# VectorE adds up 28 of wq's 32 slices, wq comes in two halves, and TensorE's code is steered by a branch and a hint

## The chip, the cores and the metric

The kernel runs on one NeuronCore of one Trainium2 chip. The metric is the device time of one execution in microseconds. Engines are named as in the profile: PE is TensorE, DVE is VectorE, ACT is ScalarE, POOL is GpSimd, SP is SyncE; a q behind the name (SPq) is its instruction queue. All data are 32-bit floats.

## The reference

One decode step: a layer norm of one token, attention over a cache of 65,536 keys, and a two-layer network with relu beside it, all added to the input.

```python
B, Sq, D = 1, 1, 512
Hq, Hkv, Sk, Dh = 32, 8, 65536, 128          # four query heads share a key head
x  = A_x
xn = layernorm(x)
q  = (xn @ wq)                               # wq: [512, 4096], 8.4 MB
scores = q . k_cache * Dh**-0.5              # k_cache: [8, 65536, 128], 268 MB
o  = softmax(scores) . v_cache               # v_cache: the same size
attention = o @ wo                           # wo: [4096, 512], 8.4 MB
mlp = relu(xn @ w1) @ w2                     # 512 x 1792 and 1792 x 512, 3.7 MB each
return x + attention + mlp
```

## The kernel before

**Storage.** Two large buffers hold what comes from memory: `ks` for K tiles and `vs` for V tiles, 64 KB in each of 128 partitions, 8.4 MB each. They are used again for the weights: wq and later wo lie in `vs`, w1 and w2 in `ks`.

**The loads.** All large transfers are issued by SP on one queue, in this order: wq in two pieces (`WQ = [4, 28]`, slices of 512 columns; the helper is `load_slices`, L157), the first K tile (L175), the first V tile (L310), then K and V tiles in turn (L305, L310), four of each for every one of the 8 key heads, 32 of each in all; at the end w1 and w2 into `ks`, and wo into `vs` in seven pieces (`WO`). A V tile is issued when its semaphore `v_free` is raised. The first V tile overwrites wq, so SP waits (L319) for `wq_read`, the mark of the last matmul that reads wq.

**The head.** After the first loads are issued, the program of the helper context ends with a barrier of the engines (L179). Then VectorE, TensorE and ScalarE compute the layer norm (L210 to L230), some constant matrices (L234 to L249), and a spread form of xn: `pz`, a small matmul (L262), has the 128 x 32 numbers that belong to the 32 slices of wq. L264 multiplies them out to `xs`, 128 x 32 x 8, in which each slice's column stands at the place of its key head. wq is laid out with (head, 16 row groups) on the partitions and, for each of the 32 slices, 512 columns in the free dimension, so that

```python
pr[32 * c : 32 * c + HKV, :] += xs[:, i, :]^T @ vs[:, i * 512 : (i + 1) * 512]     # i = 0..31, c = i % 4
```

gives all query heads: 32 matmuls of 128x512 in 32-bit floats (L288), in four row groups c of one PSUM bank. `pr` is copied to `rows` (L295), turned by four transposes (L279) and summed over c into `qall` (L297). GpSimd hands each head its four queries in `qcur` (L336).

**The loop.** TensorE runs one loop of 32 passes (`STEPS`); a pass is one K tile (32 matmuls, L352), the maximum handling (L357 to L359), and one V tile (32 matmuls, L368). VectorE has a loop of 8 heads with four tiles written out in it (L384 to L423), ScalarE one of 8 heads with the exponentials (L430). VectorE raises `k_free` when the scores of a tile are read and `v_free` when a V tile's product is done. VectorE's loop is placed with `head_slot`, which fixes the slot of a code block at which its first instruction is loaded.

**The end.** TensorE multiplies by w1, w2 and wo (L451, L513, L548), VectorE transposes the result (L560), SP stores it. VectorE's last transpose stands in a loop that runs once (`last_turn`); its closing branch carries a hint that is placed ahead of VectorE's main loop (`end_hint`). Such a hint is an instruction that names a later branch.

**Order.** Each engine runs its program in the order written. `Flow.op` gives an instruction a wait for the marks it is handed and raises the engine's own semaphore; `DV.mark` is VectorE's latest mark.

Of the kernel before, what the change touches and what calls it, by code (L numbers as in the profile page):

```python
# [10 lines left out]
ALU = mybir.AluOpType  # L11
AX = mybir.AxisListType
PSUM = bass.MemoryType.PSUM
ENG = mybir.EngineType

P = 128
D = 512
HQ, HKV, DH = 32, 8, 128
# [3 lines left out]
CT = 4  # L22
# [11 lines left out]
FB = DFF // P  # L34
R = HKV
SLICES = R * G
WQ = [4, 28]
WO = [8, 8, 8, 4, 2, 1, 1]
PAIRED = 16
DIRECT = 28  # L40
# [29 lines left out]
def attention_and_mlp_kernel(  # L70
# [28 lines left out]
    nc = tc.nc  # L99
    scale = float(DH) ** -0.5  # L100
    te, ve, se, ge, sy = nc.tensor, nc.vector, nc.scalar, nc.gpsimd, nc.sync

    def place(name, *shape, rows=P):
        return nc.alloc_sbuf_tensor(name, [rows, *shape], F32).ap()
# [5 lines left out]
    vs = place("vs", NT * KEYS)  # L110
# [5 lines left out]
    mine = place("mine", HKV)  # L116
# [1 line left out]
    eighth = place("eighth", R)  # L118

    flat_tr = tr.rearrange("p b i -> p (b i)")  # L120
    xs = flat_tr[:, : SLICES * HKV].rearrange("p (i h) -> p i h", h=HKV)
    xm = flat_tr[:, SLICES * HKV : SLICES * (HKV + 1)]
    om, spread = flat_tr[:, : R * HQ], flat_tr[:, R * HQ : 2 * R * HQ].rearrange("p (r h g) -> p r h g", r=R, h=HKV)
    heads = flat_tr[:, 2 * R * HQ : 2 * R * HQ + 2 * DH]
    st = place("st", 8)
# [25 lines left out]
    PE, DV, AC, GP = (Flow(nc, e, n) for e, n in ((te, "pe"), (ve, "dve"), (se, "act"), (ge, "pool")))  # L151
# [3 lines left out]
    def load(engine, name, dst, src, n=16):  # L155
        sem = nc.alloc_semaphore(name)
        i = engine.dma_start(dst, src)  # L157
        i.then_inc(sem, n)
        if claim:
            claim(i)  # L160
        return sem, n


    def load_slices(name, src, counts):
        marks = []
        for n in counts:
            cut = slice(len(marks) * D, (len(marks) + n) * D)
            marks += [load(sy, f"{name}{len(marks)}", vs[:, cut], src[:, cut])] * n
        return marks


    if True:
        x_in = load(se, "x_in", xT, x.rearrange("(p a) -> p a", p=P))
        wq_in = load_slices("wq", wq.rearrange("h (i r) a f -> (h i) (r a f)", r=R), WQ)
        i = sy.dma_start(ks, k[0, 0, :, : NT * KEYS])  # L175
# [3 lines left out]
    tc.compile()  # L179
    claim = None  # L180


    make_identity_marks = []

# [7 lines left out]
    for t in (acc_o, acc_z, pm):  # L192
# [34 lines left out]
    DV.op(lambda e: e.tensor_mul(st[:, 6:7], st[:, 6:7], st[:, 3:4]), DV.mark)  # L227
    DV.op(lambda e: e.tensor_scalar(st[:, 6:7], st[:, 6:7], -0.5, 1.5, op0=ALU.mult, op1=ALU.add), DV.mark)
    DV.op(lambda e: e.tensor_mul(st[:, 7:8], st[:, 5:6], st[:, 6:7]), DV.mark)
    xn_in = DV.op(lambda e: e.tensor_scalar_mul(xn, xc, st[:, 7:8]), DV.mark)  # L230


# [27 lines left out]
    )  # L260
    pz = pb[:, 1, :]
    PE.op(lambda e: e.matmul(pz[:, :SLICES], octet, xm, start=True, stop=True), DV.mark)  # L262
    xs_in = DV.op(
        lambda e: e.tensor_mul(  # L264
            xs, pz[:, :SLICES].unsqueeze(2).to_broadcast([P, SLICES, HKV]),
            mine.unsqueeze(1).to_broadcast([P, SLICES, HKV]),
        ),
        PE.mark,
    )
    DV.op(lambda e: e.memset(idg, 1.0))  # L270
    DV.op(lambda e: e.tensor_copy(idg[:, :G], ident[:G, :G]), DV.mark)
# [1 line left out]
    pr, pt = pa[:, 0, :], pb[:, 0, :]  # L273
# [8 lines left out]
        return pt.rearrange("p (j c l) -> p j c l", j=4, c=CT)  # L282

    cleared = DV.op(lambda e: e.memset(pr, 0.0))
    for i in range(SLICES):
        c = i % CT
        PE.op(
            lambda e: e.matmul(  # L288
                pr[32 * c : 32 * c + HKV, :], xs[:, i, :], vs[:, i * 512 : (i + 1) * 512],
                start=(i < CT), stop=(i >= SLICES - CT),  # L290
            ),
            cleared, xs_in, wq_in[i],
        )
    wq_read = PE.mark
    DV.op(lambda e: e.tensor_copy(rows, pr), PE.mark)  # L295
    q = turn()[:, :, :, :HKV].rearrange("p j c h -> p h j c")
# [45 lines left out]
    GP.op(lambda e: e.tensor_copy(fins[:, HKV - 1, :], fin))  # L342


    with nc.Fori(0, STEPS, engines=[ENG.PE]):
        te.wait_ge(k_in, 16).then_inc(k_in, -16)
        te.wait_ge(q_in, 1).then_inc(q_in, -1)  # L347
        for s in range(NT):
            tile_of = (pa, pb)[s // 2 % 2][:, s % 2, :]
            for c in range(CT):  # L350
                at = (s * CT + c) * TW
                i = te.matmul(tile_of[32 * c : 32 * c + 32, :], qcur, ks[:, at : at + TW], start=True, stop=True)  # L352
                if c == 0 and s in (4, 6):
                    i._wait_ge(s_dve, s // 2 - 1)
            if s % 2:
                i.then_inc(s_tiles, 1)
        te.transpose(pm[:G, :P], m, ident)._wait_ge(s_dve, 3).then_inc(s_max, 1)  # L357
        te.matmul(pm[:, P : P + G], ones[:G, :], dg[:, :G], start=True, stop=True)._wait_ge(s_dve, 4)  # L358
        te.matmul(  # L359
            pm[:, P + G : P + G + 1], rowg, dg[:, G : G + 1], start=True, stop=True  # L360
        ).then_inc(s_max, 1)
        te.sem_inc(s_dve, -4)
        te.wait_ge(v_in, 16).then_inc(v_in, -16)
        te.wait_ge(s_w, 1).then_inc(s_w, -1)  # L364
        n = NT * SUB // WIDE
        for i in range(n):
            c = i % CT
            mm = te.matmul(  # L368
                acc_o[32 * c : 32 * c + WIDE * G, :],
                wt[:, i * WIDE : (i + 1) * WIDE, :].rearrange("p b g -> p (b g)"),  # L370
                vs[:, i * 512 : (i + 1) * 512],
                start=(i < CT), stop=(i >= n - CT),
            )
        mm.then_inc(s_o, 1)


    end_hint = ve.mark_branch_hint_location()
    with nc.Fori(0, HKV, engines=[ENG.DVE], head_slot={ENG.DVE: 110}):
        for n in range(NP):
            for s in range(0, NT, 2):  # L380
                if s == NT - 2:

                    ve.wait_ge(s_tiles, NT // 2).then_inc(k_free, 1)
                i = ve.transpose(  # L384
                    tr[:, s * SUB : (s + 2) * SUB, :].rearrange("p b i -> p (b i)"),
                    (pa, pb)[s // 2 % 2].rearrange("p i k -> p (i k)"),
                )._wait_ge(s_tiles, s // 2 + 1)
                if s < 4:
                    i.then_inc(s_dve, 1)
            ve.sem_inc(s_tiles, -4)  # L390
            ve.drain()
            top = m if n == 0 else mc
            i = ve.reduce_max(top, tr[:, :, :G].rearrange("p b g -> p g b"), axis=AX.X)  # L393
            if n:
                ve.drain()
                i = ve.tensor_max(m, m, mc)  # L396
            i.then_inc(s_dve, 1)
            ve.reduce_max(mg, pm[:G, :P], axis=AX.X)._wait_ge(s_max, 1)  # L398
            ve.drain()
            ve.tensor_scalar(dg, idg, mg, -scale, op0=ALU.mult, op1=ALU.mult).then_inc(s_dve, 1)  # L400
            ve.tensor_copy(bias[:, n, :], pm[:, P : P + G + 1])._wait_ge(s_max, 2).then_inc(s_bias, 1)  # L401
            ve.sem_inc(s_max, -2)
            flat = acc.rearrange("p b d -> p (b d)")
            if n:
                ve.wait_ge(s_alpha, 1).then_inc(s_alpha, -1)
            ve.wait_ge(s_o, 1).then_inc(v_free, 1)  # L406
            if n == 0:
                ve.tensor_copy(flat, acc_o)  # L408
            else:
                ve.scalar_tensor_tensor(  # L410
                    flat, flat, alpha[:, n : n + 1], acc_o, op0=ALU.mult, op1=ALU.add
                )
            ve.sem_inc(s_o, -1)
        ve.drain()
        last = bias[:, NP - 1, :G].unsqueeze(1).to_broadcast([P, NP - 1, G])
        ve.tensor_sub(diff, last, bias[:, : NP - 1, :G]).then_inc(s_diff, 1)
        ve.tensor_mul(masked, acc, selb.unsqueeze(2).to_broadcast([P, WIDE, DH]))
        ve.wait_ge(s_alpha, 1).then_inc(s_alpha, -1)
        ve.tensor_mul(part[:, : NP - 1, :], part[:, : NP - 1, :], fac)
        ve.wait_ge(f_free, 1).then_inc(f_free, -1)  # L420
        ve.drain()
        ve.reduce_sum(fin[:, DH:], part.rearrange("p n g -> p g n"), axis=AX.X)
        ve.reduce_sum(fin[:, :DH], masked.rearrange("p b d -> p d b"), axis=AX.X).then_inc(f_out, 1)  # L423


    with nc.Fori(0, HKV, engines=[ENG.Activation]):
        for n in range(NP):
            se.wait_ge(s_bias, 1).then_inc(s_bias, -1)  # L428
            for g in range(G):
                i = se.activation(  # L430
                    wt[:, :, g], tr[:, :, g], AF.Exp, bias=bias[:, n, g : g + 1],
                    scale=scale, accum_out=part[:, n, g : g + 1],
                )
# [13 lines left out]
    for a in range(A):  # L447
        for c in range(CT):
# [4 lines left out]
                    start=(a == 0), stop=(a == A - 1),  # L453
# [74 lines left out]
    for j in range(SLICES):  # L528
        if j == SLICES - 2:

            for c in range(CT):
# [3 lines left out]
                        start=False, stop=False,  # L535
# [9 lines left out]
        else:  # L545
            for c in range(CT):
# [3 lines left out]
                        start=False, stop=(j == SLICES - 1),  # L550
                    ),
                    sw_in, wo_in[j],
                )

    turns = nc.alloc_registers("turns", engines=[ENG.DVE])
    nc.regs_mov(turns, 0)
    nc.br("last_turn", engines=[ENG.DVE])
# [43 lines left out]
```

## Time and profile before

| | before |
|---|---|
| median of 3 runs | 1303.62 us (1303.43 to 1303.95) |
| the profiled execution | 1303.08 us |
| its span, first to last instruction | 1301.8 us |
| busy: PE, DVE, ACT, POOL | 657.1, 268.5, 76.0, 4.1 us |
| moved | 561.06 MB, mean 431 GB/s |
| wq, 7168 KB piece, issue to landing | 21.4 us |
| the 32 K loads and 32 V loads, issue to landing (median) | 29.1 us |

The profile is of one execution. Its span leaves out 1.28 us of the execution's time. Rows of a timeline read: start in us, duration in us, engine, line, operation, output<-input, shapes, count, and in brackets the idle time of the engine before it and what ended it. Rows of a window table read: the window, its length, busy time and count of PE, PEld (weight loads), DVE, ACT and POOL, then the granted TensorE clock, the mean busy share of the 16 DMA engines, and GB/s; packets are booked where they start. Rows of DMA queues read: queue, kind, packets, MB, share of 16 engines' time. Rows of the chain read: start, duration, and what the end waited for.

### The profile page before, as it was taken

To read this page: it belongs to the slowest core of one execution; us is meant where nothing else is said; L and a number is where in the kernel's file an instruction comes from. 1 tells how busy PE (TensorE), PEld (TensorE's weight loads), DVE (VectorE), ACT (ScalarE), POOL (GpSimd) and SP (SyncE) were. 2 spreads that over 40 slices of the span, in tenths; PEclk is the share of its full clock that TensorE was granted. 3 is DMA by queue.
4 is the path that set the end of the run, shared out by engine and by line. 5 is a ranking of instruction groups with operands and counts; after the bars stand their busy time and mean duration, and the time that the engine had idled before them with its cause. 6 is when DMAs were issued, how large, how long until landed. Compare 5 with 4: busy or idle time off the path is not lost. (4 is left out here: it accounts for less than half of the span.)

```text
span 1301.8 us, 10655 instructions
## 1 busy us (share of the span) xinstructions
PE 657.1 (50%) x4512; PEld 184.1 (14%) x4512; DVE 268.5 (21%) x398; ACT 76.0 (6%) x292; POOL 4.1 (0%) x22
## 2 busy tenths in 40 slices
PE   3455455445445445535535544534544644544558
PEld 1111111111111111111111111111111111111112
DVE  2221122222112222112222112222112222201222
ACT  0000000000000000000000000000000000000000
POOL 0000000000000000000000000000000000000000
PEclk9677777677677677677677768777767767666769
DMA  9999999999999999999999999999999999999998
GB/s 419 419 449 421 449 421 449 419 437 433 431 439 421 449 421 449 421 449 419 437 433 427 443 421 449 421 449 421 449 419 437 433 423 447 421 449 421 449 417 360
DMA packets 11101, 561.06 MB, mean 431 GB/s; under 512 B 1492, under 2 KB 1496, under 8 KB 1880
## 3 DMA queue, kind: packets, MB, share of 16 engines
q1 hardware_dynamic: 10944, 561.00, 99.7%
q8 instruction: 3, 0.05, 0.0%
q10 hardware_dynamic: 152, 0.00, 0.0%
q14 instruction: 2, 0.02, 0.0%
HBM read 560.99 MB, written 0.00 MB: 431 GB/s over the span
## 5 line engine op out<-in xcount | busy, mean ns | idle before, releaser
L368 PE MATMUL acc_o<-vs,wt 128*16 128x512 f32 x2048 | 291.0, 732 | 183.7 <-PEq L364 183.7
L352 PE MATMUL pa<-ks,qcur 128*32 128x512 f32 x1024 | 174.8, 815 | 327.3 <-PEq L347 327.3
L384 DVE STREAM_TRANSPOSE tr<-pa 128x1024 f32<-128x1024 f32 x64 | 80.0, 1250 | 414.6 <-PE pa L352 414.6
L352 PE MATMUL pb<-ks,qcur 128*32 128x512 f32 x1024 | 137.6, 656 | 0.0
L430 ACT ACTIVATE wt<-tr,bias 128x128 f32<-128x128 f32 x128 | 64.3, 511 | 1082.4 <-ACTq L428 1082.4
L368 PEld LDWEIGHTS acc_o<-vs,wt 128*16 128x16 f32 x2048 | 69.2, 112 | 378.8 <-issue 378.8
L352 PEld LDWEIGHTS pa<-ks,qcur 128*32 128x32 f32 x1024 | 39.0, 134 | 434.2 <-issue 425.4
L410 DVE SCALAR_TENSOR_TENSOR acc<-acc,alpha,acc_o 128x512 f32<-128x512 f32 x24 | 17.9, 748 | 354.2 <-PE acc_o L368 354.2
L384 DVE STREAM_TRANSPOSE tr<-pb 128x1024 f32<-128x1024 f32 x64 | 80.0, 1250 | 47.8 <-PE pb L352 47.8
L352 PEld LDWEIGHTS pb<-ks,qcur 128*32 128x32 f32 x1024 | 41.2, 129 | 105.5 <-issue 86.3
L357 PE MATMUL pm<-ident,m 128*4 128x128 f32 x32 | 10.0, 313 | 87.7 <-DVE m L396 67.2
L408 DVE COPY acc<-acc_o 128x512 f32<-128x512 f32 x8 | 5.5, 692 | 119.7 <-PE acc_o L368 119.7
L358 PE MATMUL pm<-dg,ones 4*128 4x4 f32 x64 | 15.0, 302 | 21.4 <-DVE dg L400 21.4
L393 DVE TENSOR_REDUCE mc<-tr 128x4 f32<-128x512 f32 x24 | 24.1, 1006 | 1.8
L430 ACT ACTIVATION_READ_ACCUMULATOR wt<-tr,bias 128x1 f32 x128 | 23.9, 187 | 0.0
L357 PEld LDWEIGHTS pm<-ident,m 128*4 128x4 f32 x32 | 2.6, 81 | 116.8 <-DVE m L396 89.0
L358 PEld LDWEIGHTS pm<-dg,ones 4*128 4x128 f32 x64 | 12.2, 236 | 28.8 <-DVE dg L400 28.8
L288 PE MATMUL pa<-vs,tr 128*8 128x512 f32 x64 | 10.3, 803 | 8.3 <-DMA vs<-wq 7.0
L359 PE MATMUL pm<-dg,rowg 4*128 4x1 f32 x64 | 14.3, 290 | 0.0
L359 PEld LDWEIGHTS pm<-dg,rowg 4*128 4x128 f32 x64 | 13.0, 249 | 0.0
L398 DVE TENSOR_REDUCE mg<-pm 4x1 f32<-4x128 f32 x32 | 8.9, 279 | 13.0 <-PE pm L357 13.0
L401 DVE COPY bias<-pm 128x5 f32<-128x5 f32 x32 | 5.2, 164 | 27.9 <-PE pm L359 27.9
(98 smaller groups left out, 104.6 us busy)
## 6 DMA issues: line engine op xcount, KB each, us to landing
vs<-wq SPq DMA_DIRECT2D x1, 7168.0 KB, 21.4
ks<-w SPq DMA_DIRECT2D x2, 3584.0 KB, 21.7
vs<-wo SPq DMA_DIRECT2D x3, 2048.0 KB, 17.4
vs<-wq SPq DMA_DIRECT2D x1, 1024.0 KB, 4.9
vs<-wo SPq DMA_DIRECT2D x1, 1024.0 KB, 23.9
ks<-k SPq DMA_DIRECT2D x32, 29.1
vs<-v SPq DMA_DIRECT2D x32, 29.1
vs<-wo SPq DMA_DIRECT2D x1, 512.0 KB, 24.7
```

The source lines that it names most:

```text
L288: lambda e: e.matmul(pr[32 * c : 32 * c + HKV, :], xs[:, i, :], vs[:, i * 512 : (i + 1) * 512], start=(i < CT), stop=(i >= SLICES - CT),),
L352: i = te.matmul(tile_of[32 * c : 32 * c + 32, :], qcur, ks[:, at : at + TW], start=True, stop=True)
L357: te.transpose(pm[:G, :P], m, ident)._wait_ge(s_dve, 3).then_inc(s_max, 1)
L358: te.matmul(pm[:, P : P + G], ones[:G, :], dg[:, :G], start=True, stop=True)._wait_ge(s_dve, 4)
L359: te.matmul(pm[:, P + G : P + G + 1], rowg, dg[:, G : G + 1], start=True, stop=True).then_inc(s_max, 1)
L368: mm = te.matmul(acc_o[32 * c : 32 * c + WIDE * G, :], wt[:, i * WIDE : (i + 1) * WIDE, :].rearrange("p b g -> p (b g)"), vs[:, i * 512 : ...
L384: i = ve.transpose(tr[:, s * SUB : (s + 2) * SUB, :].rearrange("p b i -> p (b i)"), (pa, pb)[s // 2 % 2].rearrange("p i k -> p (i k)"),)._ ...
L393: i = ve.reduce_max(top, tr[:, :, :G].rearrange("p b g -> p g b"), axis=AX.X)
L398: ve.reduce_max(mg, pm[:G, :P], axis=AX.X)._wait_ge(s_max, 1)
L408: ve.tensor_copy(flat, acc_o)
L410: ve.scalar_tensor_tensor(flat, flat, alpha[:, n : n + 1], acc_o, op0=ALU.mult, op1=ALU.add)
L430: i = se.activation(wt[:, :, g], tr[:, :, g], AF.Exp, bias=bias[:, n, g : g + 1], scale=scale, accum_out=part[:, n, g : g + 1],)
```

## The change

- `WQ` becomes `[16, 16]`: wq is loaded in two halves.
- VectorE adds up the first 28 slices (`SUMMED`): `qsum`, 128 x 512, is cleared, and each slice is multiplied by its column of `xs` (now 128 x 32, one number for each partition and slice) and added. The 28 instructions are two loops with four slices in a pass (`TURN`), over 16 and 12 slices; the addresses of the slice and of the column come from the loop's register, and a drain stands in front of each.
- TensorE keeps slices 28 to 31 as before (with `xh`, the spread form for these four), and one matmul of `qsum` by `mine` (the 0/1 matrix of head membership) adds the sum into the first row group.
- TensorE branches at the head, right behind the barrier, to a block `far` whose code stands behind its main loop, and back.
- At TensorE's end stands a loop that runs once (`last_round`), with a register addition and a branch whose hint (`pe_hint`) is placed ahead of TensorE's main loop.
- VectorE's hint moves from its main loop to the layer norm, and `head_slot` is dropped.

```diff
-WQ = [4, 28]
+WQ = [16, 16]
+SUMMED = 28
+TURN = 4
...
-    xs = flat_tr[:, : SLICES * HKV].rearrange("p (i h) -> p i h", h=HKV)
-    xm = flat_tr[:, SLICES * HKV : SLICES * (HKV + 1)]
+    xs, qsum = flat_tr[:, :SLICES], flat_tr[:, SLICES : SLICES + 512]
+    xm = flat_tr[:, SLICES + 512 : 2 * SLICES + 512]
+    xh = flat_tr[:, 2 * SLICES + 512 : 2 * SLICES + 512 + (SLICES - SUMMED) * HKV].rearrange(
+        "p (i h) -> p i h", h=HKV
+    )
...
     claim = None
+    hop = nc.cur_bb
+    hops = nc.alloc_registers("hops", engines=[ENG.PE])
+    nc.regs_mov(hops, 0)
+    te.br_lt(hops, 1, on_true="far", on_false="near")
+    nc.switch_bb("near")
...
     DV.op(lambda e: e.tensor_mul(st[:, 7:8], st[:, 5:6], st[:, 6:7]), DV.mark)
+    end_hint = ve.mark_branch_hint_location()
     xn_in = DV.op(lambda e: e.tensor_scalar_mul(xn, xc, st[:, 7:8]), DV.mark)
...
-    xs_in = DV.op(
+    DV.op(lambda e: e.tensor_copy(xs, pz[:, :SLICES]), PE.mark)
+    xh_in = DV.op(
         lambda e: e.tensor_mul(
-            xs, pz[:, :SLICES].unsqueeze(2).to_broadcast([P, SLICES, HKV]),
-            mine.unsqueeze(1).to_broadcast([P, SLICES, HKV]),
-        ),
-        PE.mark,
+            xh, pz[:, SUMMED:SLICES].unsqueeze(2).to_broadcast([P, SLICES - SUMMED, HKV]),
+            mine.unsqueeze(1).to_broadcast([P, SLICES - SUMMED, HKV]),
+        )
     )
...
     cleared = DV.op(lambda e: e.memset(pr, 0.0))
-    for i in range(SLICES):
+    DV.op(lambda e: e.memset(qsum, 0.0))
+
+    def add_slices(first, last):
+        DV.need(wq_in[first])
+        with nc.Fori(first // TURN, last // TURN, engines=[ENG.DVE]) as t:
+            for i in range(TURN):
+                at = t * TURN + i
+                ve.drain()
+                ve.scalar_tensor_tensor(
+                    qsum, vs[:, bass.ds(at * 512, 512)], xs[:, bass.ds(at, 1)], qsum, op0=ALU.mult, op1=ALU.add
+                )
+
+    add_slices(0, WQ[0])
+    add_slices(WQ[0], SUMMED)
+    ve.drain()
+    DV.op(lambda e: e.memset(st[:, 0:1], 0.0))
+    for i in range(SUMMED, SLICES):
         c = i % CT
         PE.op(
             lambda e: e.matmul(
-                pr[32 * c : 32 * c + HKV, :], xs[:, i, :], vs[:, i * 512 : (i + 1) * 512],
-                start=(i < CT), stop=(i >= SLICES - CT),
+                pr[32 * c : 32 * c + HKV, :], xh[:, i - SUMMED, :], vs[:, i * 512 : (i + 1) * 512],
+                start=True, stop=(c > 0),
             ),
-            cleared, xs_in, wq_in[i],
+            cleared, xh_in, wq_in[i],
         )
+    PE.op(lambda e: e.matmul(pr[:HKV, :], mine, qsum, start=False, stop=True), DV.mark)
     wq_read = PE.mark
...
+    pe_hint = te.mark_branch_hint_location()
     with nc.Fori(0, STEPS, engines=[ENG.PE]):
...
         mm.then_inc(s_o, 1)
-    end_hint = ve.mark_branch_hint_location()
-    with nc.Fori(0, HKV, engines=[ENG.DVE], head_slot={ENG.DVE: 110}):
+    nc.br("far_end", engines=[ENG.PE])
+    with nc.body("far", parent=hop, valid_engines=[ENG.PE]):
+        te.drain()
+        nc.br("near", engines=[ENG.PE])
+    nc.switch_bb("far_end")
+    with nc.Fori(0, HKV, engines=[ENG.DVE]):
...
+    rounds = nc.alloc_registers("rounds", engines=[ENG.PE])
+    nc.regs_mov(rounds, 0)
+    nc.br("last_round", engines=[ENG.PE])
+    with nc.body("last_round", valid_engines=[ENG.PE]):
+        nc.regs_alu(rounds, rounds, 1, op=ALU.add)
+        te.br_lt(rounds, 1, on_true="last_round", on_false="last_rounded").branch_hint(pe_hint)
+    nc.switch_bb("last_rounded")
```

## The prediction

> **What bounds the kernel now.** I read the page first (slices, queues), then the chain that ended last, the DMA queues by window, the timeline of both ends, and stage windows of the last microseconds.
>
> ```profile
> span 1301.8 us, 10655 instructions
> DMA  9999999999999999999999999999999999999998
> q1 hardware_dynamic: 10944, 561.00, 99.7%
> q8 instruction: 3, 0.05, 0.0%
> q14 instruction: 2, 0.02, 0.0%
> ```
>
> All forty slices have the DMA engines at 9 tenths or more (8 in the last), and queue q1 alone fills 99.7% of sixteen engines' span. The kernel is a stream of 561 MB. Only three things can change its time: when the stream starts, holes in it, and what follows its last byte. Five packets of the stream's span are instruction code: three of about 16 KB on q8 and two of about 8 KB on q14. The chain that ended last shows how the end hangs on the stream:
>
> ```profile
> 1272.90 23.92 DMA vs<-wo
> 1296.86 1.16 PE acc_z L513 x8
> 1298.05 0.70 DVE rows L544
> 1298.80 0.40 PE acc_y L533 x8
> 1299.19 0.68 PE acc_y L548 x16
> 1299.89 0.41 DVE yt L560
> ```
>
> From a landing of wo at 1296.82 on, nothing waits for anything but this chain. Moving that landing moves the end one for one. The windows of the last microseconds (the two last columns are DMA share and GB/s) show that the sixteen engines do not finish together:
>
> ```profile
> 1296.00:1297.00 1.00, 0.39 (x8) 0.10 (x8) 0.00 (x0) 0.00 (x0) 0.00 (x0) 1.00 1.05 395
> 1297.00:1297.40 0.40, 0.40 (x8) 0.00 (x0) 0.00 (x0) 0.00 (x0) 0.00 (x0) 1.00 0.75 251
> 1297.40:1297.90 0.50, 0.50 (x8) 0.00 (x0) 0.00 (x0) 0.00 (x0) 0.00 (x0) 1.00 0.20 78
> 1297.90:1298.40 0.50, 0.27 (x13) 0.26 (x16) 0.35 (x1) 0.00 (x0) 0.00 (x0) 1.00 0.13 49
> 1298.40:1298.90 0.50, 0.46 (x20) 0.16 (x12) 0.34 (x1) 0.00 (x0) 0.00 (x0) 1.00 0.10 37
> ```
>
> A share of 0.20 is three engines, 0.13 two, 0.10 between one and two. Twelve are done by 1297.4, and two go on to 1298.9, 1.5 us later. When the code came is read from the DMA queues of four windows, 45 to 48, 48 to 1270, 1273 to 1276 and 1290 to 1299 us, in this order:
>
> ```profile
> q8 instruction: 1, 0.02, 2.0%
> ...
> q1 hardware_dynamic: 9189, 529.64, 100.1%
> ...
> q8 instruction: 1, 0.02, 2.3%
> ...
> q8 instruction: 1, 0.02, 0.8%
> ```
>
> One 16 KB fetch falls in TensorE's first pass of its loop, none in the 31 passes after it (the middle window lists no code), one behind the loop, the third after 1290. I infer, and no row names the engine, that the two fetches before the end are what the two late engines had to carry; q14's two account for the engines about 0.5 us late.
>
> **The head.** Its timeline, in three pieces, and the windows around the first V load:
>
> ```profile
> 0.75 0.86 SPq L157 DMA_DIRECT2D vs<-wq  x2
> 2.98 0.17 DVE L186 MEMSET ones<- 128x128 f32 x1 [2.98 <-PEq L179]
> 6.04 0.58 PE L211 MATMUL pm<-st,ones 128*128 128x1 f32 x2 [6.04 <-DVE st L210]
> 11.58 0.18 DVE L256 TENSOR_TENSOR tr<-eighth,xn 128x32 f32<-128x32 f32 x1
> 12.49 0.42 DVE L264 TENSOR_TENSOR tr<-pb,mine 128x256 f32<-128x256 f32 x1 [0.73 <-PE pb L262]
> 12.97 0.16 DVE L271 COPY idg<-ident 4x4 f32<-4x4 f32 x1
> 13.23 0.48 DVE L284 MEMSET pa<- 128x512 f32 x1
> 22.64 8.44 PE L288 MATMUL pa<-vs,tr 128*8 128x512 f32 x56 [6.98 <-DMA vs<-wq]
> 31.66 0.35 SPq L310 DMA_DIRECT2D vs<-v  x1
> 33.12 0.19 POOL L336 COPY qcur<-qall 128x4 f32<-128x4 f32 x1 [29.52 <-DVE qall L297]
> 42.27 3.64 PE L352 MATMUL pa<-ks,qcur 128*32 128x512 f32 x16 [9.62 <-PEq L347]
> ...
> 1.00:2.00 1.00, 0.00 (x0) 0.00 (x0) 0.00 (x0) 0.00 (x0) 0.00 (x0) 1.00 0.41 66
> 40.00:41.00 1.00, 0.00 (x0) 0.00 (x0) 0.00 (x0) 0.00 (x0) 0.00 (x0) 0.50 0.00 0
> 41.00:42.00 1.00, 0.00 (x0) 0.00 (x0) 0.00 (x0) 0.00 (x0) 0.00 (x0) 0.50 2.43 1049
> ```
>
> The V load writes over wq, so it is issued (31.66) only after wq's last matmul (22.64 + 8.44 = 31.08, so 0.58 later). It is not needed until the K load in front of it is through: the windows book packets where they start, and 1049 GB/s for 1 us is sixteen packets of 64 KB, one for each engine, in 41 to 42. I take 41.4 for the changeover. From issue to bytes takes about 0.9 us (0.75 to the first bytes in 1 to 2). The slack of the V load's issue is therefore 41.4 - 0.9 - 31.66 = 8.8 us. That is the cover under which everything on wq is free, and the change spends it.
>
> **The change part by part.**
>
> *wq in two halves.* Still two issues on SP, the same bytes ahead of the same K load: 0. The first half is half of what landed at 22.6, so about 12.5 by proportion; VectorE comes later than that anyway.
>
> *VectorE's head.* L264 (0.42) becomes a copy (0.16 as L271) and a product over 128x32 (0.18 as L256): with an issue gap about even. A second 128x512 memset, 0.48 as L284. Loop entry, 0.2 as an estimate. L284 ended at 13.71, so the first sum starts at 13.71 + 0.48 + 0.2 = 14.4 (rounding down the even part).
>
> *28 sums one behind the other.* Nearest rows: the same operation with an accumulator of the same size, and the instruction behind it across a drain; then K loads whose address comes from a register (52) and from a constant (1213), each with the VectorE transpose that starts at the same release:
>
> ```profile
> 188.79 0.75 DVE L410 SCALAR_TENSOR_TENSOR acc<-acc,alpha,acc_o 128x512 f32<-128x512 f32 x1 [15.54 <-PE acc_o L368]
> 189.61 0.17 DVE L416 TENSOR_TENSOR diff<-bias 128x12 f32<-128x12 f32 x1
> ...
> 52.19 1.25 DVE L384 STREAM_TRANSPOSE tr<-pb 128x1024 f32<-128x1024 f32 x1 [0.58 <-PE pb L352]
> 52.32 0.34 SPq L305 DMA_DIRECT2D ks<-k  x1
> ...
> 1213.62 0.33 SPq L305 DMA_DIRECT2D ks<-k  x1
> 1213.62 1.25 DVE L384 STREAM_TRANSPOSE tr<-pb 128x1024 f32<-128x1024 f32 x1 [0.58 <-PE pb L352]
> ```
>
> One sum is 0.75, and the drain costs 0.07 (189.61 - 188.79 - 0.75): 0.82. Behind each drain stands the register work for two addresses (slice and scalar), which nothing covers because the sum cannot start before it. No row shows it on VectorE. Bounds: 0 below; above 0.26, twice the 0.13 by which a register address delays SP's issue (52.32 - 52.19 against 0.00). I take 0.12, one such address, since both come from one index and can share the work. So 0.94 each (bounds 0.82 and 1.08). [...] The sums end at 14.4 + 28 x 0.94 = 40.7 (37.4 to 44.6). The wait for the second half is covered: it lands at 22.6, VectorE gets there at 29.
>
> [...]
>
> *Behind the sums.* Drain and the small memset 0.2, TensorE's one matmul on the sum 0.6 (as the cold L211), to the V issue 0.58, to bytes 0.9: 2.3. V's bytes start at 43.0, 1.6 after 41.4: a hole in the stream, and all later loads move by it. Queued behind that wait on SP are all K and V loads. q comes 33.12 - 31.08 = 2.0 after the matmul, at about 43.6 in place of 33.1; TensorE waits for it 1.3 past 42.27. The next K load goes out some 10 us after that start (52.32 in the rows above), and V takes as long as K did (42.27 - 22.64 = 19.6): hidden.
>
> *TensorE's shorter head, the branch and the two hints.* 28 fewer matmuls in front of the loop move the loop and the tail forward in the code. The branch touches code behind the loop right after the barrier (2.98), so the 16 KB that came at 46 should come at about 3 to 4. It sits in front of the matmul that waits until 6.04: 3 us of cover for a stall, and if the cover goes, everything in the head moves by the excess. The fetch still falls inside the stream (from 1.7), but the hole at 41.4 lets its engine catch up. [...] Gain: the two late engines end with q14's, at about 1297.85 in place of 1298.9: 1.05. Bounds: 0 (the fetches only move) and 1.5 (all code out of the stream). I take 1.05, since nothing touches q14's engines for certain.
>
> *head_slot gone, VectorE's hint earlier, more VectorE code.* A further 8 KB fetch would make one more engine 0.5 late, which is not later than q14's: 0. One instruction more in VectorE's head, below 0.1: inside the rounding.
>
> **The sum.** +1.6 - 1.05 = +0.55. The profiled execution took 1303.08 (span 1301.8), the median is 1303.62: I put the difference on the median, 1304.2. A measurement tells about 0.2% (2.6 us) from no change.
>
> **The rivals.**
> 1. *The sums fit.* Register work of 0.07 or less: 0.89 each, end by 39.3, no hole worth naming. But then the early fetch's engine does not catch up, which costs some of the gain: -0.2 to -1.2, 1302.4 to 1303.4. For it: most of SP's 0.13 may be SP's own. Against: two addresses, not one.
> 2. *The other side: register work becomes the bound of the head.* At 0.26 the sums end at 14.4 + 28 x 1.08 = 44.6, V starts at 46.9, 5.5 late: +4.5, 1308.1. It decides (slower by over 2.6) from a hole of 3.65 on, that is sums of 1.01 us, 0.19 of register work. For it: one sequencer does it bare behind each drain, 28 times. [...]
> 3. *The branch does not do what it says.* [...] If the branch or the hint fails, the fetches stay: no gain, +1.6, 1305.2; a stall at the branch past 6.04 could add 1 to 2.
>
> **How the numbers follow.** Forecast (sums of 0.90 to 1.01, 1303.3 to 1306.2) 0.50; sums fit 0.18; register-bound 0.24; fetches stay with a hole as forecast 0.08. Time 1304.2, the forecast's. Range 1302.5 to 1307.3: it leaves out the upper half of rival 2 (0.13) and a little of rival 1. Faster by over 0.2% needs more than all code fetches are worth: 0.02. Slower: rival 2 and a part of rival 3: 0.25. Within: 0.73.
>
> **What would show it.** 28 scalar_tensor_tensor of 0.75 us from about 14.4, some 0.94 apart, the last done near 40.7; the V load issued near 42.1; no packets starting between about 41.4 and 43; the first score matmul near 43.7; q8 with one packet before 10 us and none from 45 to 1290; by the last windows no engine over 0.6 us behind the rest. The forecast is wrong if sums are over 1.0 or under 0.9 us apart, or if a q8 packet stays behind 1270.

## The result, and the profile after

The changed kernel takes 1316.64 us (median of 5 runs, 1316.38 to 1316.72) where the kernel before took 1303.43 beside it: a ratio of 1.0102, interval 1.0091 to 1.0114. It is 13.2 us slower. The prediction said 1304.2 and at most 1307.3. The profiled execution took 1316.67 us, span 1315.2. Line numbers have moved: L220 is the old L210 (first use of x), L304 the sums, L321 TensorE's matmul on their sum, L338 the V load (old L310).

The page of the changed kernel, to be held against the first fence of the prediction:

```profile
span 1315.2 us, 10666 instructions
DMA  9699999999999999999999999999999999999998
GB/s 413 257 442 419 446 433 429 444 417 446 431 431 440 421 446 427 435 440 421 446 427 435 440 421 446 421 440 438 423 446 415 446 437 425 446 415 446 435 421 357
q1 hardware_dynamic: 10944, 561.00, 98.7%
q8 instruction: 2, 0.03, 0.0%
```

Same bytes, but the second slice (32.9 to 65.8 us) is down to 6 tenths and 257 GB/s. All else is as full as it was. The loss is one hole near the start, and the end has only moved with it. The chain that ended last:

```profile
1286.05 24.19 DMA vs<-wo
...
1313.36 0.41 DVE yt L601
```

The landing of wo comes at 1310.24 in place of 1296.82, 13.42 later; from there to the end of yt it is 3.5 us in both. So the tail is unchanged and the whole loss is in the landing. Now the head, from the timeline of the changed kernel:

```profile
0.75 0.86 SPq L162 DMA_DIRECT2D vs<-wq  x2
0.76 0.41 ACTq L162 DMA_DIRECT2D xT<-x  x1
14.52 0.16 DVE L220 TENSOR_REDUCE st<-xT 128x1 f32<-128x4 f32 x1 [9.38 <-DMA xT<-x]
23.10 0.75 DVE L304 SCALAR_TENSOR_TENSOR tr<-vs,tr 128x512 f32<-128x512 f32 x1 [0.24 <-issue]
...
37.42 0.75 DVE L304 SCALAR_TENSOR_TENSOR tr<-vs,tr 128x512 f32<-128x512 f32 x1 [0.20 <-issue]
38.82 0.75 DVE L304 SCALAR_TENSOR_TENSOR tr<-vs,tr 128x512 f32<-128x512 f32 x1 [0.64 <-issue]
...
49.59 0.75 DVE L304 SCALAR_TENSOR_TENSOR tr<-vs,tr 128x512 f32<-128x512 f32 x1 [0.20 <-issue]
50.56 1.87 PE L321 MATMUL pa<-tr,mine 128*8 128x512 f32 x2 [24.47 <-DVE st L311]
52.89 0.35 SPq L338 DMA_DIRECT2D vs<-v  x1
55.27 3.42 PE L381 MATMUL pa<-ks,qcur 128*32 128x512 f32 x16 [0.93 <-PEq L376]
```

The surprise stands in the third row, before the first sum: VectorE waits 9.38 us for x and starts the layer norm at 14.52. In the kernel before, the same wait was 0.69 us:

```profile
5.83 0.16 DVE L210 TENSOR_REDUCE st<-xT 128x1 f32<-128x4 f32 x1 [0.69 <-DMA xT<-x]
```

Everything up to the first sum moved by the same 8.69 us (23.10 - 8.69 = 14.41, the start that the prediction had). The hole itself, in windows of the changed kernel (last two columns: DMA share and GB/s booked where packets start):

```profile
40.00:41.00 1.00, 0.00 (x0) 0.00 (x0) 0.80 (x2) 0.00 (x0) 0.00 (x0) 1.00 0.15 66
...
52.00:53.00 1.00, 0.44 (x1) 0.00 (x0) 0.53 (x1) 0.00 (x0) 0.00 (x0) 1.00 0.00 0
53.00:54.00 1.00, 0.78 (x4) 0.72 (x4) 0.16 (x1) 0.00 (x0) 0.00 (x0) 1.00 1.73 590
```

The last K packet starts before 41, the first V packet after 53. That is the hole which the prediction expected at 1.6 us.

**Why x was late.** x is 2 KB. The DMA issues of the kernel before, with KB each and us from issue to landing, and how many packets of wq's queue (q1) and of x's (q10) started from 2 to 5 us:

```profile
vs<-wq SPq DMA_DIRECT2D x1, 1024.0 KB, 4.9
xT<-x ACTq DMA_DIRECT2D x1, 2.0 KB, 5.0
...
q1 hardware_dynamic: 137, 1.33, 108.7%
q10 hardware_dynamic: 121, 0.00, 2.3%
```

The same for the changed kernel, with the packets of 5 to 7 and 7 to 9 us:

```profile
vs<-wq SPq DMA_DIRECT2D x2, 4096.0 KB, 18.2
xT<-x ACTq DMA_DIRECT2D x1, 2.0 KB, 13.7
...
q1 hardware_dynamic: 24, 0.79, 91.3%
q10 hardware_dynamic: 24, 0.00, 0.7%
...
q1 hardware_dynamic: 31, 1.02, 118.9%
...
q10 hardware_dynamic: 31, 0.00, 0.9%
```

24 against 24, 31 against 31: the two queues take turns, one packet of x for one packet of wq. x goes out as 128 rows of 16 bytes, by an even spread eight for each of 16 engines, and each waits for one packet of wq. A packet of wq is one partition's part of the piece: 8 KB (0.23 MB over 28 from 2 to 3 us in the kernel before) for four slices, 32 KB (0.79 MB over 24) for sixteen. Four times the packet, and x's wait grows from 5.0 to 13.7 us.

### The profile page after: what moved, and what is told of

The parts are those of the page before. It is cut to its first block, busy times and chain, and to the rows that moved or that the text cites. A ratio compares the mean times of both kernels' runs of the same rounds, so it can differ in the third digit from the quotient of the medians.

```text
span 1315.2 us, 10666 instructions
## 1 busy us (share of the span) xinstructions
PE 661.6 (50%) x4458; PEld 185.9 (14%) x4458; DVE 290.0 (22%) x429; ACT 76.0 (6%) x292; POOL 4.1 (0%) x22
## 5 line engine op out<-in xcount | busy, mean ns | idle before, releaser
L397 PE MATMUL acc_o<-vs,wt 128*16 128x512 f32 x2048 | 297.2, 745 | 177.3 <-PEq L393 177.3
L304 DVE SCALAR_TENSOR_TENSOR tr<-vs,tr 128x512 f32<-128x512 f32 x28 | 21.0, 752 | 6.4 <-issue 6.4
L321 PE MATMUL pa<-tr,mine 128*8 128x512 f32 x2 | 1.9, 1040 | 24.5 <-DVE st L311 24.5
L388 PEld LDWEIGHTS pm<-dg,rowg 4*128 4x128 f32 x64 | 13.7, 262 | 0.0
```

The source lines that it names most:

```text
L304: ve.scalar_tensor_tensor(qsum, vs[:, bass.ds(at * 512, 512)], xs[:, bass.ds(at, 1)], qsum, op0=ALU.mult, op1=ALU.add)
L388: te.matmul(pm[:, P + G : P + G + 1], rowg, dg[:, G : G + 1], start=True, stop=True).then_inc(s_max, 1)
L397: mm = te.matmul(acc_o[32 * c : 32 * c + WIDE * G, :], wt[:, i * WIDE : (i + 1) * WIDE, :].rearrange("p b g -> p (b g)"), vs[:, i * 512 : ...
```

## The experiments

The kernel before took 1303.05 to 1303.16 us beside these runs. Each profile was also read for two moments: when the V load is issued, and when wo lands, which is start plus duration of wo's load in the chain that ended last (before: 31.66 and 1296.82).

**A smaller first piece.** The changed kernel with the first piece of four slices again:

```diff
-WQ = [16, 16]
+WQ = [4, 12, 16]
-        DV.need(wq_in[first])
+        DV.need(*wq_in[first:last])
-    add_slices(0, WQ[0])
-    add_slices(WQ[0], SUMMED)
+    add_slices(0, 16)
+    add_slices(16, SUMMED)
```

> The changed kernel with wq in pieces of 4, 12 and 16 slices in place of 16 and 16, so that the first packets are 8 KB as before. Theory 1 (x's small packets take turns with wq's on every DMA engine, and each waits for a wq packet, so x is late by wq's packet size): VectorE's first sum over x starts near 5.8 us in place of 14.5, the sums run from 14.4 to 41.7, the V load is issued at 44.2 in place of 52.9, and the time falls by 8.7 us, to about 1308. Theory 2 (the code fetch of TensorE's branch at the head, a packet at 7.6 us, holds x up): x stays at 13 to 14.5 and the time at 1316.6.

1308.31 us, ratio 1.0039 [1.0025, 1.0053]. From its timeline:

```profile
5.83 0.16 DVE L220 TENSOR_REDUCE st<-xT 128x1 f32<-128x4 f32 x1
6.05 0.58 PE L221 MATMUL pm<-st,ones 128*128 128x1 f32 x2 [6.05 <-DVE st L220]
14.66 0.75 DVE L304 SCALAR_TENSOR_TENSOR tr<-vs,tr 128x512 f32<-128x512 f32 x1 [0.49 <-DMA vs<-wq]
```

x is back at 5.83, the sums start at 14.66, V is issued at 44.43, and some 8 of the 13 us are back. What is left, the sums and the matmul behind them, still costs about 5.

**Halves alone.** The kernel before with wq in halves and nothing else:

```diff
-WQ = [4, 28]
+WQ = [16, 16]
```

> The kernel before with one line changed: wq in halves of 16 slices. Theory 1: x's first use moves from 5.8 to about 13 to 14.5 us; wq's matmuls start near 22.6 as soon as their operand and the first half allow and all 32 are done near 31, the V load is issued within 1.5 us of 31.7, under its slack of 8.8, and the time stays within 0.7 us of 1303.4. Theory 2: x stays at 5.8, time the same. Either way the halves alone cost nothing; x's row tells the theories apart.

1303.2 us, ratio 1.0 [0.999, 1.0009]. From its timeline:

```profile
13.06 0.16 DVE L210 TENSOR_REDUCE st<-xT 128x1 f32<-128x4 f32 x1 [7.93 <-DMA xT<-x]
21.01 8.86 PE L288 MATMUL pa<-vs,tr 128*8 128x512 f32 x64 [1.32 <-DVE pa L284]
```

x is late here too (13.06), yet TensorE still ends its matmuls (32, each listed as two) at 29.9 and V is issued at 30.44. In this kernel the halves are free. The prediction costed them in the kernel before and carried the zero over to one where the path from x to V had no slack left.

**A piece of eight.** The kernel before with `WQ = [8, 24]`.

> The kernel before with wq in pieces of 8 and 24 slices, so that the first packets are 16 KB. If each of x's eight small packets for an engine waits for one wq packet, x's first use goes from 5.8 (8 KB, 0.31 us each) through here 8.3 (0.61 us each) to 13.1 (32 KB, 1.22 us each): linear in the packet's time. If x only comes behind the whole first piece, it would be at 9.5 (5.8 plus the 1 MB that the piece is longer by, 2.4 us, and again as much for 2 MB: 10.6 at most). The time stays at 1303.

1302.86 us in one run. Its timeline and its DMA issues:

```profile
8.17 0.16 DVE L210 TENSOR_REDUCE st<-xT 128x1 f32<-128x4 f32 x1 [3.03 <-DMA xT<-x]
```

```profile
vs<-wq SPq DMA_DIRECT2D x1, 2048.0 KB, 7.2
xT<-x ACTq DMA_DIRECT2D x1, 2.0 KB, 7.4
```

x at 5.83, 8.17 and 13.06 us with packets of 8, 16 and 32 KB: 2.34 us for the first 8 KB more, 4.89 for the next 16, close to a straight line. That x lands just behind the first piece (7.4 and 7.2) is no queueing behind all of it, by which 9.5 or more was expected: x and the piece have 128 packets each, by an even spread eight on each engine, and take turns to the end (60 of x against 63 of wq from 2 to 5 us).

**x ahead of wq, sums written out.** The changed kernel with x on SP's queue in front of wq, halves kept, and the 28 sums unrolled with constant addresses:

```diff
-        x_in = load(se, "x_in", xT, ...)
+        x_in = load(sy, "x_in", xT, ...)
-        with nc.Fori(first // TURN, last // TURN, engines=[ENG.DVE]) as t:
-            for i in range(TURN):
-                at = t * TURN + i
+        for at in range(first, last):
...
```

> After with x's load on SP's queue ahead of wq (wq stays in halves of 16) and the 28 sums written out with constant addresses. x no longer takes turns with wq: it should be used by 5.3, when VectorE is through with its memsets; sums from about 13.9, V issued at 48.53 - 9.2 = 39.3 to 40. The stream starts 0.4 us later, by one issue on SP. By turn-taking: 1303.5 to 1305, about 11 under after; if something other than the order of x and wq held x back (the size of the first piece itself), x stays near 14.5 and it is 1312 as before.

1305.69 us, ratio 1.0023 [1.0014, 1.0032]. Its DMA issues, and its timeline:

```profile
vs<-wq SPq DMA_DIRECT2D x2, 4096.0 KB, 18.1
xT<-x SPq DMA_DIRECT2D x1, 2.0 KB, 1.6
```

```profile
5.52 0.15 DVE L220 TENSOR_REDUCE st<-xT 128x1 f32<-128x4 f32 x1
14.76 23.04 DVE L302 SCALAR_TENSOR_TENSOR tr<-vs,tr 128x512 f32<-128x512 f32 x28 [0.91 <-DMA vs<-wq]
38.02 1.87 PE L319 MATMUL pa<-tr,mine 128*8 128x512 f32 x2 [11.61 <-DVE st L309]
40.35 0.35 SPq L336 DMA_DIRECT2D vs<-v  x1
```

With the same halves x lands 1.6 us after its issue. It was the order of the queues and not the size of the piece in itself. The second row also shows the first half of wq landing at 14.7, not at the 12.5 that the prediction had by proportion; once x is early, the first sum waits 0.91 for it. Without that wait V would have been out at 39.44, where it was expected.

**Written out alone.** The same unrolling on the changed kernel, x left where it was.

> The changed kernel with the 28 sums written out with constant addresses in place of two loops with register addresses. If the 0.20 us between the sums are 0.07 of drain and 0.13 of register work, the step falls from 0.955 to 0.82, the sums take 23.0 in place of 27.2 us (with the loops' own stops), the V load is issued 4.2 us earlier, near 48.7, and the time falls to about 1312.4. If the drain itself takes the 0.20 (a rival in which the register work is hidden), the step stays at 0.95 and the time falls by the 0.9 us of the loops' stops at most.

1312.23 us, ratio 1.0069 [1.0053, 1.0086]. From its timeline:

```profile
22.94 23.04 DVE L302 SCALAR_TENSOR_TENSOR tr<-vs,tr 128x512 f32<-128x512 f32 x28
48.53 0.35 SPq L336 DMA_DIRECT2D vs<-v  x1
```

28 sums take 23.04, 0.82 a step, against 27.24 (23.10 to 50.34) in the loop: register addresses and loop cost 4.2 us, and the time came down by 4.4. In the loop a step is 0.955 (24 equal ones); the rest is one stop of 0.44 between the two loops (0.64 against 0.20 in the row at 38.82) and two of 0.13, at the two back edges of the second loop; the three of the first loop cost nothing.

**Small piece and written out.** Both mends together, `WQ = [4, 12, 16]` and the 28 sums unrolled.

> The changed kernel with both causes of the hole eased: wq in pieces of 4, 12 and 16, and the 28 sums written out with constant addresses. First sum near 14.6, 28 steps of 0.82, the V load issued near 40.3, inside its slack of 8.8 us behind 31.7. If the hole is all that made the change slower, the time is back at 1303.2, within 0.7; if something else in the change costs (a rival), it stays above 1304.

1305.52 us, ratio 1.0018 [1.0009, 1.0028]. V is issued at 40.58, where it was expected, but the time does not come back: the slack ends before 40.5. The next two runs, and those above, place its end.

**24 and 20 sums.** `WQ = [4, 12, 16]`, the loops kept, and four or eight more slices left to TensorE.

```diff
-SUMMED = 28
+SUMMED = 24        # and 20
-                start=True, stop=(c > 0),
+                start=(i < SUMMED + CT), stop=(c > 0 and i >= SLICES - CT),
```

> After with pieces of 4, 12 and 16 slices and 24 sums instead of 28 (eight slices go to TensorE). Between the run with 16 sums (V issued at 31.93) and the one with 28 (44.43) lie 1.04 us a sum, so V should be issued near 40.3. Where does the V load's slack end? Theory 1, the prediction's 40.5: no hole, level with before (1303.1, within 0.5). Theory 2, what the runs so far line up on (time over before is V's issue less some 39.5): 0.8 over, 1303.9. Theory 3, a late V costs a fixed amount as soon as it is late at all, as the written-out run (40.58, +2.5) would have it: 1305.5.

> The same with 20 sums: V issued near 36.1, 4 us inside the slack by theories 1 and 2: 1303.1 (within 0.5). If it is over 1304, the slack ends far earlier than any of the theories say.

24 sums: 1304.65 us, 1.0014 [1.0005, 1.0023], V issued at 40.59. 20 sums: 1303.23, 1.0002 [0.9993, 1.0012], V issued at 35.76. The changed kernel and its variants in order of V's issue, one profiled execution of each:

| | V issued | wo lands | later than before |
|---|---|---|---|
| 16 sums (below) | 31.93 | 1297.03 | 0.21 |
| 20 sums | 35.76 | 1296.83 | 0.01 |
| x first, written out | 40.35 | 1298.43 | 1.61 |
| small piece, written out | 40.58 | 1298.70 | 1.88 |
| 24 sums | 40.59 | 1299.58 | 2.76 |
| small piece | 44.43 | 1301.85 | 5.03 |
| written out | 48.53 | 1306.00 | 9.18 |
| no steering (below) | 51.45 | 1308.93 | 12.11 |
| no hint (below) | 52.72 | 1310.20 | 13.38 |
| changed kernel | 52.89 | 1310.24 | 13.42 |

In the five late ones, issue minus loss is 39.40, 39.35, 39.34, 39.34 and 39.47: a slack that ends at 39.4, and one us lost for each us behind it. Near the bend the loss is 0.7 to 1.6 more than this line. The engines do not come to their last K packet together: in the changed kernel's window from 40 to 41 one packet of 64 KB starts alone (66 GB/s for 1 us), where the kernel before starts none. Such a spread would round the bend; that it accounts for these sizes is not shown. The 1.15 between three runs with V within 0.25 us proves little: repeated executions of each of these three kernels lie 2 to 3.5 us apart, and by their medians the order is the other way, with 24 sums 1.6 over the kernel before, and the two written-out ones 2.5 and 2.6.

**No steering.** The changed kernel without the branch, the far block and the one-turn loop with its hint.

> The changed kernel without TensorE's branch at the head, its block behind the loop, and the one-turn loop with its hint. Theory 1: x still lands at 12.4 to 14.5 us (at most the 1.2 to 2 us that a 16 KB code packet holds one engine are gained), the code fetch moves from 7.6 us to TensorE's first pass of its loop (56 to 60 us), the time is 1314.5 to 1316.8. Theory 2: x back at 5.8, time near 1308.

1314.96 us, ratio 1.009 [1.0073, 1.0106], 1.7 less than with them. From its timeline:

```profile
13.09 0.16 DVE L215 TENSOR_REDUCE st<-xT 128x1 f32<-128x4 f32 x1 [7.95 <-DMA xT<-x]
```

x comes at 13.09 in place of 14.52, as it does with halves alone (13.06): with the early code fetch in the head, x is 1.43 later. The branch brings it and not the hint: without the hint (below) x is at 14.36. So the steering did not gain the predicted 1.05. Here it cost about 1.4.

**Sixteen sums.** `WQ = [4, 12, 16]` and `SUMMED = 16`, steering kept: V's issue (31.93) is as early as before, so what the steering is worth stands alone.

> The changed kernel with wq in pieces of 4, 12 and 16 and only the first 16 slices added by VectorE; the other 16 stay on TensorE. The V load is then issued near 34, inside its slack, so no hole is left and what remains is the worth of the code steering. Theory 1 (a code fetch counts only if its engine is the last one at the end; the fetch behind the loop, at 1285 to 1294 us, is still there and still sets the end): 1303.2, within 0.5 of the kernel before. Theory 2 (the step of the prediction: the steering is worth 1.05 us): 1302.1.

1303.14 us, ratio 1.0003 [0.9994, 1.0012]: nothing.

**A branch past the loop.** The kernel before with the early branch alone, its far block put behind the w1 matmuls, so that both of TensorE's fetches come early:

```diff
...
+    te.br_lt(hops, 1, on_true="far", on_false="near")
+    nc.switch_bb("near")
...
+    with nc.body("far", parent=hop, valid_engines=[ENG.PE]):     # behind the w1 matmuls
+        te.drain()
+        nc.br("near", engines=[ENG.PE])
...
```

> The kernel before with one branch of TensorE right behind the barrier to a block whose code stands behind the w1 matmuls of its end, and back; nothing else. If the branch brings that block and the next one at the head, the q8 packets at 46 and 1274 us both move to the first 12 us. TensorE may wait for the block past 6.04 us; the V load has 8.8 us of slack for that. Theory 1 (each fetch leaves its engine 1.4 us behind for good, wherever it falls in the stream): no gain, 1302.7 to 1303.4. Theory 2 (fetches at the head are free): the two late engines at the end are gone and the time falls by about 1.0 us, to 1302.1.

1302.91 us, ratio 0.9998 [0.9989, 1.0007]. From its timeline:

```profile
10.14 0.59 PE L215 MATMUL pm<-st,ones 128*128 128x1 f32 x2 [10.14 <-issue]
32.60 0.35 SPq L314 DMA_DIRECT2D vs<-v  x1
```

Its windows from 5 to 9 and from 12 to 16 us list one 16 KB packet of code each, and the one from 16 to 1290 none of that size (it has two of 8 KB). Both fetches are in the head, and TensorE's first matmul comes at 10.14 (6.04 in the kernel before), though VectorE starts on x at 5.66. The row names no releaser (`<-issue`); that TensorE stalled there for its code is an inference from the two packets. V is 0.94 later, inside its slack. And with both fetches moved the time is the same. The prediction's rival 3 had named a stall at the branch, of 1 to 2 us, for the changed kernel, and there it did not come: with the small first piece, which has the changed kernel's branch and x early, TensorE's first matmul is at 6.05, as in the kernel before.

**No hint.** The changed kernel without TensorE's one-turn loop; the branch stays.

> After without TensorE's one-turn loop at the end and its hint; the early branch stays. Theory 1, the hint does nothing here: 1316.6 (within 0.6), code fetches at about 7.6 and 1294, none behind that. Theory 2, the hint is what took the third code fetch away: a 16 KB fetch comes back at about 1310, and the end is up to 0.5 us later.

1317.87 us (1316.86 to 1318.19), ratio 1.0111 [1.0095, 1.0127]. The interval of the changed kernel's ratio overlaps this one, though all four runs lie above its five (1316.72 at most). The DMA view of its last microseconds, and of the changed kernel's:

```profile
q8 instruction: 1, 0.02, 1.2%
...
y<-yt SPq DMA_DIRECT2D x1, 2.0 KB, 3.1
```

```profile
y<-yt SPq DMA_DIRECT2D x1, 2.0 KB, 1.4
```

A 16 KB code fetch is back at the very end, and in the profiled execution it ran beside the store of the result, which took 3.1 us in place of 1.4: 1.7 us on the end, with the chain up to yt the same. So theory 2 has its fetch, at a higher price than the 0.5 it named. But the hint is not the whole of it: two kernels above have the hint and one 16 KB packet at the end all the same (the small piece behind 1305.0, with y taking 3.2 us, and 20 sums behind 1298.2, with y at 1.4). What decides on this last fetch stays open.

## Why the prediction was wrong, point by point

- *The stream bounds the kernel and wo's landing sets the end*: right. 13.42 of landing is the loss, and the tail behind it kept its 3.5 us.
- *wq in two halves: 0*: this step failed. It looked at the bytes and at the first half's landing, not at what else is in the engines' queues then. x, 2 KB beside 32 KB packets, came 8.69 us later, 1.43 of which need the early code fetch; with the small piece x was back at 5.83.
- *The sums start at 14.4*: right behind x (14.41 after taking off the 8.69); the 0.2 taken for the loop's entry is a gap of 0.24 in the row at 23.10.
- *0.94 a sum*: right as a step (0.955 measured; 0.82 with constant addresses, so register work is 0.13 and not 0.12). The 28 sums took 27.24 instead of 26.3, 0.94 more: most of it is the stop between the loops (0.44) and two smaller ones (0.13 each), for which the sum has no term, the rest the step. Rival 2, slower by register work at 0.26, pointed to the right side for a wrong reason.
- *Behind the sums 1.38 to V's issue*: 2.55 measured, 1.17 more. The matmul took 1.87, not 0.6: the row taken for it, L211, streams one column, while this one streams 512. The prediction's own row at 42.27 had the price: 16 such matmuls in 3.64, 0.9 for four, which overlap (the page of before has 815 ns as the mean of one), and the sum's matmul is listed as two.
- Together V's issue: 8.69 + 0.94 + 1.17 = 10.8 late, 52.89 for 42.1.
- *Slack until 40.5*: it ended at 39.4, 1.1 earlier. Part of it is in the windows above: from 53 to 54 nine V packets of 64 KB start (590 GB/s for 1 us) with a share of 1.73 of sixteen engines, so 3.1 us each (1.73 x 16 / 9); the sixteen from 41 to 42 of before had a share of 2.43, 2.4 us each. So the stream that starts again loses 0.6 us on its first packets. Without steering the sixteen from 52.4 to 53.2 have a share of 3.79 over 0.8 us, 3.0 us each. The other 0.5 stays open.
- *Steering: -1.05*: 0. No run shows this gain, not even the one with both fetches in the head (1302.91). In the changed kernel the first fetch moved (46 to about 7.6) and one at the end went, but the one behind the loop stayed:

```profile
q8 instruction: 1, 0.02, 1.5%
...
q8 instruction: 1, 0.02, 1.4%
```

These are the code queue of the changed kernel from 5 to 9 us and from 1291 to 1296. The prediction named that second packet as what would show it wrong. Its inference of one late engine for each fetch fits the ends of the runs, and so does the catching up in the hole: about 1.1 us behind wo's landing two engines are still busy in the kernel before (share 0.13, 1297.9 to 1298.4), two also with both fetches in the head and no hole (0.15) and without steering, where nothing moves the first fetch ahead of the hole (0.14), and one in the changed kernel:

```profile
1311.50:1312.00 0.50, 0.46 (x16) 0.31 (x16) 0.50 (x1) 0.00 (x0) 0.00 (x0) 1.00 0.06 25
```

So a fetch that is only moved within the full stream still leaves its engine late, and the one late engine that is left ends no earlier than two did: the way from wo's landing to yt stayed at 3.5 us. What the end would gain with no engine late, no run shows.

The errors add up: 10.8 + 1.1 + 1.05 = 12.95 on a forecast of 0.55 gives 13.5, against 13.42 measured.

## What to carry to other kernels

Before a large load is cut differently, look at every small load that is in flight beside it: here a transfer of many tiny packets took turns with the other queue (24 to 24, 31 to 31), so that it waited for as many large packets as it had small ones (13.7 us in place of 5.0), and its consumer is where the price showed. A step that is free in a kernel with slack isn't free in one where another part of the same change spends that slack; the path has to be added up again from its first input. For a matmul's price take a row with the same number of streamed columns (here 0.58 us for one column, 1.87 for 512, both listed as two). No version here beats the kernel before by more than can be measured.

## What the runs showed of the hardware that was not expected

- The queues of x and wq alternated packet by packet: 24 to 24, 31 to 31; x's 2 KB load took 5.0, 7.4 and 13.7 us beside packets of 8, 16 and 32 KB (12.3 for the last without the early code fetch, from its issue at 0.76 to its first use at 13.09), and 1.6 us ahead of them.
- With a 16 KB code fetch in the head x was 1.43 us later (13.09 to 14.52), and with one beside the last store that store took 1.7 us longer (1.4 to 3.1). At the end the shares are those of one late engine for each fetch that had no hole in the stream behind it (0.13 to 0.15 for two, 0.06 for one); no row names the engine.
- The first 64 KB packets of a stream that had run dry took 3.1 us (changed kernel) and 3.0 us (no steering) in place of 2.4 (kernel before, 41 to 42).
- Two register addresses from one index cost VectorE 0.13 us for each instruction behind a drain (0.955 against 0.82), no more than SP's one (0.13, 52.32 against 52.19).
